# Linear attention through W' = blockdiag(kv) wo and r = pq/den, in a fused transformer block with its gradients

## The chip, the cores and the metric

One Trainium2 chip, one core of it. The kernel is one launch that computes the output of a block and six gradients. The metric is the device time of one execution in microseconds (us); the kernel before takes 846.03 us (median of 3 runs, 845.99 to 848.4). Profiles are of one execution; their span is 1.7 to 1.9 us shorter than the time of the same run.

## The reference

Everything is bf16, S = 2048 rows, D = 640, H = 32 heads of 20 columns, F = 1728.

```python
def A(x, wqkv, wo):                      # linear attention, not causal
    q, k, v = heads(x @ wqkv)
    phi = lambda t: where(t > 0, t + 1, exp(t)) + 1e-6
    pq, pk = phi(q), phi(k)
    kv  = einsum("hsd,hse->hde", pk, v)  # 20 x 20 for each head
    z   = pk.sum(rows)
    num = einsum("hqd,hde->hqe", pq, kv)
    den = einsum("hqd,hd->hq", pq, z) + 1e-6
    return merge(num / den) @ wo

h   = x + A(layernorm(x), wqkv, wo)
out = h + swiglu(layernorm(h), w1, w3, w2)
# returned: out and, for a given grad_out, the gradients of x, wqkv, wo, w1, w3, w2
```

## The kernel before

The program order of every engine is fixed by hand. Rows are handled in 16 tiles of 128. The stages are: setup (layernorm, k, and M = pk^T xn with one more column of ones, which gives z), a fill (the late tiles of q, the first attention tiles), the MLP, its weight gradients, the backward attention with the gradient of h, and last the gradients of wqkv and x. The parts that the change touches:

```python
# fill and MLP: num and den in one product with kvbd (20 columns of kv and 1 of z for each head)
def f2_nd(t):
    for m, a, b, bank, off, first in ND:
        T.matmul(nd[t][bank][:, ...], lhsT=pqT[:, m, tile t], rhs=kvbd[:, m, a * DA:b * DA], ...)
def f2_o(t):                                  # o = num / den, on VectorE
    V.tensor_scalar(out=den, in0=<column of den>, scalar1=1e-6, op0=ALU.add)      # twice
    V.reciprocal(out=rden[:, t, :], in_=den)
    V.tensor_tensor(out=o_t, in0=<num>, in1=rden of the head, op=ALU.mult)         # twice
def f2_ot(t):                                 # o transposed: tiles 0-3 on TensorE, later ones by DMA
    ...
def f2_at(t):                                 # h = x + o wo
    T.matmul(at, lhsT=oT[t][:, c, :], rhs=wo[:, c, half], ...)

def q_late(t):
    pq = p1.tile([P, D], BF16, name="pq", bufs=4)
    ...                                       # two products, ScalarE exp and relu, two VectorE operations
    dma(out=pq_d[tile t], in_=pq)

# backward attention, per tile
def b_go(t):     # g_h wo^T; times rden -> gnd; gnd * o, summed per head -> one more column of gnd
def b_gndT(t):   # gnd transposed
def b_gkv(t):    # gkv += pq^T gnd, five small products, in PSUM over all tiles
def b_gpq(t):    # g_q = phi'(q) * (gnd kvbd^T), six small products
def wo_parts():  # gradient of wo = o^T g_h, stored directly
# last stage: kvbd's gradient transposed by TensorE (13 blocks of 128 x 128), g_v's weights gm,
# g_k and the products for the gradient of wqkv ("jobs"), then the gradient of x
```

Of the kernel before, what the change touches and what calls it, by code (L numbers as in the profile page):

```python
# [9 lines left out]
P = 128  # L10
# [10 lines left out]
DA = DH + 1  # L21
C, CP = H * DA, 768
ST, DT, CT = S // P, D // P, CP // P
# [14 lines left out]
M_W = [(b - a) * DA for a, b in M_H]  # L38
M_MAX = max(M_W)
KV_SLOT = [(0, 0), (0, M_W[0]), (0, M_W[0] + M_W[1]), (1, 0), (1, M_W[3])]  # L40

C_H = [_heads(cc * P, min(C, (cc + 1) * P), DA) for cc in range(CT)]
SPLIT_D, SPLIT_C = 19, 18
# [13 lines left out]
ND = _pieces(M_H, SPLIT_D, DA)  # L57
GP = _pieces(C_H, SPLIT_C, DH)


SQ = _pieces(M_H, SPLIT_D, DH)
SQ_BLOCKS = [(c, [m for m in range(DT) if M_H[m][0] * DH < (c + 1) * P and M_H[m][1] * DH > c * P]) for c in range(DT)]
BLOCKS = [(cc, list(range(a * DH // P, (b * DH - 1) // P + 1))) for cc, (a, b) in enumerate(C_H)]
# [3 lines left out]
def kernel(  # L67
# [34 lines left out]
    pq_d = dram.tile([S, D], BF16, name="pq_d")  # L102
# [3 lines left out]
    o_d = dram.tile([S, D], BF16, name="o_d")  # L106
# [3 lines left out]
    pq_v, pk_v, xn_v, o_v, hn_v, m_v = rows(pq_d), rows(pk_d), rows(xn_d), rows(o_d), rows(hn_d), rows(m_d)  # L110
# [9 lines left out]
    x_ext = U1.tile([P, ST, D + 2], BF16, name="x_sb", tag="S0")  # L120
    x_sb = x_ext[:, :, 0:D]
# [12 lines left out]
    kvbd = cp.tile([P, DT, CP], BF16, name="kvbd")  # L134
# [54 lines left out]
    mask = cp.tile([P, DT, M_MAX], BF16, name="mask")  # L189

    def make_mask(m):
        a, b = M_H[m]
        v = mask[:, m, 0:M_W[m]]
        V.memset(v, 1.0)
        v = v.rearrange("p (h e) -> p h e", e=DA)

        G.affine_select(out=v, in_=v, pattern=[[-DH, b - a], [0, DA]], compare_op=ALU.is_ge, fill=0.0,
                        base=m * P - a * DH, channel_multiplier=1)
        G.affine_select(out=v, in_=v, pattern=[[DH, b - a], [0, DA]], compare_op=ALU.is_gt, fill=0.0,
                        base=a * DH + DH - m * P, channel_multiplier=-1)  # L200

# [12 lines left out]
    def load_pqT(c):  # L214
        dmaT(out=pqT[:, :, c * W:(c + 1) * W], in_=pq_d[c * W:(c + 1) * W, :])

# [8 lines left out]
    pk_all = p1.tile([P, ST, D], BF16, name="pk_all")  # L225
    mT = p1.tile([P, DT, D], BF16, name="mT")
    Z = p1.tile([P, DT], F32, name="Z")
# [37 lines left out]
    def phi(acc, dst, then=None):  # L265

        mq, rq = (p1.tile([P, D], BF16, name=n, bufs=4) for n in ("mq", "rq"))
        A.activation(two(mq[:]), acc[:, :, 0:HD], AF.Exp)
        A.activation(two(rq[:]), acc[:, :, 0:HD], AF.Relu)  # L269

        def rest():
            V.tensor_scalar(out=mq[:], in0=mq[:], scalar1=1.0, scalar2=1e-6, op0=ALU.min, op1=ALU.add)
            V.tensor_tensor(out=dst, in0=mq[:], in1=rq[:], op=ALU.add)
            if then is not None:
                then()
        held.append(rest)
# [5 lines left out]
    def q_store(t, pq):  # L282
        dma(out=pq_v[:, t, :], in_=pq)

    def q_tile(t):
        pq = p1.tile([P, D], BF16, name="pq", bufs=4)
        phi(p1_mm(t, 0), pq[:], lambda: q_store(t, pq[:]))
# [21 lines left out]
    def m_part(m, tiles):  # L309
        if m not in macc:  # L310
            macc[m] = [ps.tile([P, 512], F32, name="macc", tag=("m", "tr")[m % 2], bufs=2) for _ in range(2)]
        for t in tiles:
            for j, n in enumerate((HD, HD + 1)):
                T.matmul(macc[m][j][:, 0:n], lhsT=pk_all[:, t, m * P:(m + 1) * P],  # L314
                         rhs=x_ext[:, t, j * HD:j * HD + n], start=(t == 0), stop=(t == ST - 1))

    def m_end(m):
# [4 lines left out]
        V.tensor_copy(out=Z[:, m:m + 1], in_=acc[1][:, HD:HD + 1])  # L322
# [3 lines left out]
    def kv_block(m, acc):  # L326

        a, b = M_H[m]
        n = (b - a) * DH
        for c in range(DT):  # L330
            T.matmul(acc[:, 0:n], lhsT=mT[:, c, m * P:(m + 1) * P],
                     rhs=wqkv[:, c, 2 * D + a * DH:2 * D + b * DH], start=(c == 0), stop=(c == DT - 1))
        kv, mk = (x[:, m, y].rearrange("p (h e) -> p h e", e=DA)
                  for x, y in ((kvbd, slice(a * DA, b * DA)), (mask, slice(0, M_W[m]))))
        V.tensor_tensor(out=kv[:, :, 0:DH], in0=acc[:, 0:n].rearrange("p (h e) -> p h e", e=DH),
                        in1=mk[:, :, 0:DH], op=ALU.mult)
        V.tensor_scalar(out=kv[:, :, DH], in0=mk[:, :, DH], scalar1=Z[:, m:m + 1], scalar2=None, op0=ALU.mult)

    def zero_pads():
        V.memset(w2T[:, :, F:FP], 0.0)  # L340
        V.memset(x_ext[:, :, D:D + 2], 1.0)
# [38 lines left out]
    for t in range(ST):  # L380
# [11 lines left out]
        phi_rest()  # L392
        phi(k, pk_all[:, t, :])
# [19 lines left out]
    phi_rest()  # L413
    group_out(SC - 1)
    for m in range(DT):
        V.memset(kvbd[:, m, :], 0.0)
        make_mask(m)

    def p1_kv(m):
        kv_block(m, ps.tile([P, 2, 512], F32, name="kvp", tag="big", bufs=2)[:, 0])  # L420
# [5 lines left out]
    m_part(1, (14, 15))  # L426
    m_end(1)
    q_tile(5)
    phi_rest()
    q_tile(6)  # L430
    phi_rest()
    q_tile(7)
    phi_rest()
    m_part(2, range(ST))
    m_end(2)
    m_part(3, range(ST))
    m_end(3)
    load_pqT(0)
    p1_kv(0)
    m_part(4, range(8))  # L440
    p1_kv(1)
    m_part(4, range(8, ST))
    m_end(4)
    load_pqT(1)
    ps.release()
    load_x(0, 2)
    load_x(2, 4)
# [5 lines left out]
    nd, oT, hn, hnT, hhT = {}, {}, {}, {}, {}  # L453

    def f2_nd(t):
        nd[t] = [ps.tile([P, 512], F32, name="nd", bufs=2) for _ in range(2)]
        for m, a, b, bank, off, first in ND:
            a0 = M_H[m][0]
            T.matmul(nd[t][bank][:, off:off + (b - a) * DA], lhsT=pqT[:, m, t * P:(t + 1) * P],
                     rhs=kvbd[:, m, a * DA:b * DA], start=first, stop=True, skip_group_check=True)  # L460

    def f2_o(t):
        o_t = pf.tile([P, D], BF16, name="o_t", bufs=2)
        den = pf.tile([P, H], F32, name="den", bufs=2)
        halves = ((0, SPLIT_D, nd[t][0]), (SPLIT_D, H, nd[t][1]))
        del nd[t]
        seg = [n[:, 0:(b - a) * DA].rearrange("p (h e) -> p h e", e=DA) for a, b, n in halves]
        for (a, b, _), s in zip(halves, seg):
            V.tensor_scalar(out=den[:, a:b], in0=s[:, :, DH], scalar1=1e-6, scalar2=None, op0=ALU.add)
        V.reciprocal(out=rden[:, t, :], in_=den[:])  # L470
        for (a, b, _), s in zip(halves, seg):
            V.tensor_tensor(out=o_t[:, a * DH:b * DH].rearrange("p (h d) -> p h d", d=DH), in0=s[:, :, 0:DH],
                            in1=rden[:, t, a:b].unsqueeze(2).to_broadcast([P, b - a, DH]), op=ALU.mult)
        oT[t] = o_t

    def f2_ot(t):
        if t >= TPC:
            o_t, oT[t] = oT[t], pf.tile([P, DT, P], BF16, name="oT", bufs=2)
            dmaT(out=oT[t][:], in_=o_t[:])
            dma(out=o_v[:, t, :], in_=o_t[:])  # L480
            return
        dma(out=o_v[:, t, :], in_=oT[t][:])
        tr = ps.tile([P, DT, P], BF16, name="tr", bufs=1)
        for c in range(DT):
            T.transpose(tr[:, c, :], oT[t][:, c * P:(c + 1) * P], ident[:])
        oT[t] = pf.tile([P, DT, P], BF16, name="oT", bufs=2)
        A.copy(out=oT[t][:], in_=tr[:])

    def f2_at(t, tag="nd"):
        on_pe = t < 2 * TPC  # L490
        for j in range(2):
# [4 lines left out]
            for c in range(DT):  # L496
                T.matmul(at[:, 0:HD], lhsT=oT[t][:, c, :], rhs=wo[:, c, j * HD:(j + 1) * HD],  # L497
# [7 lines left out]
    def q_late(t):  # L505

        mq, rq = (p1.tile([P, D], BF16, name=n, bufs=4) for n in ("mq", "rq"))
        pq = p1.tile([P, D], BF16, name="pq", bufs=4)
        for j in range(2):
            acc = ps.tile([P, 512], F32, name="mm", bufs=3)  # L510
# [5 lines left out]
        V.tensor_tensor(out=pq[:], in0=mq[:], in1=rq[:], op=ALU.add)  # L516
        q_store(t, pq[:])
# [6 lines left out]
    def f2_ht(t):  # L524
# [7 lines left out]
        tr = ps.tile([P, DT, P], BF16, name="trh", tag="mm", bufs=3)  # L532
# [4 lines left out]
    def mm5(w, fc, rhs):  # L537
        return mm5_to(ps.tile([P, W], F32, name="mm", bufs=3), w, fc, rhs)
# [7 lines left out]
    def mlp_ghh(n):  # L546
        if n < SC * FT:
            ghh_chunk(n, ps.tile([P, W], F32, name="mm", bufs=3))
# [87 lines left out]
    def f2_ndo(t):  # L636
        f2_nd(t)
        f2_o(t)

    FILL = 8  # L640

    def f2_kv(m):
        kv_block(m, ps.tile([P, 512], F32, name="mm", bufs=3))
# [7 lines left out]
    for f, t in ((q_late, 8), (f2_kv, 2), (q_late, 9), (q_late, 10), (f2_kv, 3), (mlp_ghh, 4), (f2_kv, 4), (f2_ndo, 0), (q_late, 11),  # L651
                 (f2_ot, 0), (f2_ndo, 1), (q_late, 12), (f2_at0, 0), (f2_ot, 1), (f2_ndo, 2), (f2_hn, 0), (q_late, 13),
                 (f2_at0, 1), (f2_ot, 2), (f2_ht, 0), (f2_ndo, 3), (f2_hn, 1), (q_late, 14), (f2_x, 4), (f2_at0, 2),
                 (f2_ot, 3), (w2T_rest, 8 * P), (f2_ht, 1), (mlp_ghh, 5), (f2_hn, 2), (f2_at0, 3), (q_late, 15),
                 (f2_ht, 2), (f2_hn, 3), (f2_ndo, 4), (mlp_ghh, 6), (f2_ot, 4), (f2_x, 6), (f2_ht, 3), (load_g2T, 1),
# [643 lines left out]
```

## Time and profile before

| what | us |
|---|---|
| time, median | 846.03 |
| span of the profiled run | 844.2 |
| first matmul of the MLP starts at | 102.5 |
| first product of wo's gradient starts at | 559.7 |
| first product of the jobs on g_q starts at | 587.5 |
| first product of the x gradient starts at | 649.6 |

TensorE is the limit nearly everywhere; the prediction shows the busy table, the slices and the chain. This is TensorE's list of waits; the columns are what waited and for what, then us in total, times, and the longest one.

```profile
PE tr L245 <- DVE x_sb L156: 6.6, 3, 5.4
PE at L497 <- DMA oT<-o_t: 0.7, 1, 0.7
```

Behind the first tiles' layernorm nothing costs TensorE even a microsecond. The next line is a window: bounds, length, busy us and instructions of PE, weight loads, VectorE, ScalarE and GpSimd, then the clock, the share of DMA engines in use and GB/s.

```profile
587.50:649.60 62.10, 61.59 (x497) 45.15 (x495) 29.66 (x46) 13.48 (x34) 0.00 (x0) 1.00 0.81 178
```

### The profile page before, as it was taken

What the parts mean: (1) busy time and instruction counts of PE and PEld (TensorE: products, weight loads), DVE (VectorE), ACT (ScalarE), POOL (GpSimd) and SP (SyncE); (2) the same over time, 40 slices, a digit from 0 to 9 for tenths busy, and PEclk for the clock granted to TensorE, in tenths of its full rate; (3) what the DMA queues carried; (4) which work ended last, traced back from release to release, by engine and by line L of the source; (5) the groups of instructions that cost most, each with busy time, mean ns of one, the idle gap of its engine ahead of it and who ended that gap; (6) DMA issues with size and microseconds to landing.
All of it is one profiled execution on the core that took longest, in us unless ns stands there. A gap on an engine that the chain in (4) does not pass through costs nothing.

```text
span 844.2 us, 14506 instructions
## 1 busy us (share of the span) xinstructions
PE 831.2 (98%) x5719; PEld 534.1 (63%) x5719; DVE 415.0 (49%) x952; ACT 321.0 (38%) x606; POOL 33.3 (4%) x55
## 2 busy tenths in 40 slices
PE   6999999999999999999999999999999999999998
PEld 4667654555555555777777777777777777555554
DVE  7853788778687657400046665662562545200000
ACT  5864877655655666011121112122211333311111
POOL 2310100000000000001000000000000000000000
PEclk9999999999999999999999999999999999999999
DMA  9999799566455457999768789749696688686661
GB/s 263 305 311 231 212 226 262 167 173 173 126 144 148 122 185 211 214 247 267 218 172 188 183 196 218 162 100 239 150 228 116 139 205 178 137 184 147 162 165 37
DMA packets 341156, 158.57 MB, mean 188 GB/s; under 512 B 241760, under 2 KB 339808, under 8 KB 341088
## 3 DMA queue, kind: packets, MB, share of 16 engines
q1 hardware_dynamic: 312272, 144.67, 69.3%
q10 hardware_dynamic: 28816, 12.97, 6.7%
q8 instruction: 45, 0.74, 0.4%
q14 instruction: 23, 0.19, 0.1%
HBM read 48.64 MB, written 50.32 MB: 117 GB/s over the span
## 4 chain that ended last, share of the span: by engine, by line
PE 95%; DMA 2%; DVE 2%; ACT 1%; issue 0%; SPq 0%; DVEq 0%; ACTq 0%
PE mm L293 19%; PE job L1093 19%; PE ghn L858 14%; PE gxn L1226 8%; PE o L622 7%; PE gw L797 7%; PE big L251 4%; PE at L497 3%; PE macc L314 3%; PE gwo L965 3%; PE h L915 3%; PE dkv L1173 2%; DMA x_sb<-in_A_x_dram 1%; PE mm L251 1%; PE h L946 1%; PE gkv L938 1%
## 5 line engine op out<-in xcount | busy, mean ns | idle before, releaser
L1093 PE MATMUL job<-gb,hnN 128*128 128x432 bf16 x640 | 117.0, 346 | 0.0
L858 PEld LDWEIGHTS <-ggb 128*128 128x128 bf16 x864 | 83.1, 98 | 30.9
L1093 PEld LDWEIGHTS <-hnN 128*128 128x128 bf16 x640 | 62.6, 98 | 54.1
L293 PE MATMUL mm<-pqT,w 128*128 128x512 bf16 x405 | 95.6, 379 | 0.0
L293 PEld LDWEIGHTS <-w 128*128 128x128 bf16 x540 | 52.5, 98 | 60.5
L1097 ACT CAST obs<-job 128x432 bf16<-128x432 f32 (+1 forms) x60 | 29.1, 485 | 134.8 <-PE job L1093 134.8
L622 PE MATMUL o<-w,hhT 128*128 128x320 bf16 x448 | 67.5, 299 | 0.0
L858 PE MATMUL ghn<-w13a,ggb 128*128 128x320 bf16 x448 | 65.6, 299 | 0.0
L293 PE MATMUL mm<-g2T,w2T 128*128 128x512 bf16 x260 | 64.6, 379 | 0.2 <-ACT up L570 0.2
L858 PE MATMUL ghn<-w13b,ggb 128*128 128x320 bf16 x416 | 63.5, 299 | 0.0
L622 PEld LDWEIGHTS <-hhT 128*128 128x128 bf16 x448 | 43.8, 98 | 23.6
L797 PE MATMUL gw<-g,hb 128*128 128x320 bf16 x416 | 57.7, 299 | 0.0
L881 ACT ACTIVATE y<-wb,s,ln_rs 128x640 bf16<-128x640 f32 x32 | 29.4, 920 | 66.5 <-DVE wb L877 66.5
L303 ACT CAST ghh<-mm 128x512 bf16<-128x512 f32 x52 | 30.5, 586 | 55.3 <-PE mm L293 53.9
L797 PEld LDWEIGHTS <-hb 128*128 128x128 bf16 x416 | 40.3, 98 | 15.3
L1226 PE MATMUL gxn<-wqT,gT 128*128 128x320 bf16 x320 | 48.7, 299 | 0.0
L869 ACT ACTIVATE gs<-ghn 128x640 bf16<-128x640 f32 x16 | 11.2, 703 | 87.4 <-PE ghn L858 87.4
L562 ACT ACTIVATE sig<-mm 128x512 bf16<-128x512 f32 x56 | 33.5, 598 | 28.3 <-PE mm L293 26.0
L293 PEld LDWEIGHTS <-w2T 128*128 128x128 bf16 x280 | 27.2, 98 | 25.4 <-issue 0.5
L251 PEld LDWEIGHTS <-pqT 128*128 128x128 bf16 x320 | 31.7, 101 | 14.9 <-issue 1.4
L251 PE MATMUL big<-wqkv,pqT 128*128 128x320 bf16 x240 | 38.7, 314 | 0.3 <-ACT rq L269 0.2
L1093 PEld LDWEIGHTS <-g 128*128 128x128 bf16 x320 | 31.2, 98 | 12.3 <-issue 0.3
(158 smaller groups left out, 1157.3 us busy)
## 6 DMA issues: line engine op xcount, KB each, us to landing
hh_d<-hhT SPq DMA_DIRECT2D x24, 256.0 KB, 2.6
gg_d<-gate SPq DMA_DIRECT2D x24, 256.0 KB, 2.6
gg_d<-up SPq DMA_DIRECT2D x24, 256.0 KB, 2.5
ggb<-gg_d SPq DMA_DIRECT2D x6, 896.0 KB, 6.1
ggb<-gg_d SPq DMA_DIRECT2D x6, 832.0 KB, 7.7
out_dram<-obs ACTq DMA_DIRECT2D x40, 108.0 KB, 2.2
ggb<-gg_d SPq DMA_DIRECT2D x2, 1728.0 KB, 12.4
x_sb<-in_A_x_dram SPq DMA_DIRECT2D x5, 640.0 KB, 4.9
```

The lines of the kernel that those rows point to most:

```text
L251: T.matmul(acc, lhsT=pqT[:, c, t * P:(t + 1) * P], rhs=wqkv[:, c, n0:n0 + HD], start=(c == 0), stop=(c == DT - 1))
L293: T.matmul(acc[:], lhsT=w[:, c, fc * P:(fc + 1) * P], rhs=rhs[:, c, :], start=(c == 0), stop=(c == DT - 1))
L303: A.copy(out=ghh[n // 2][:, n % 2, :], in_=acc[:])
L314: T.matmul(macc[m][j][:, 0:n], lhsT=pk_all[:, t, m * P:(m + 1) * P], rhs=x_ext[:, t, j * HD:j * HD + n], start=(t == 0), stop=(t == ST - 1))
L562: A.activation(sig[:, i, :], gp[:], AF.Sigmoid)
L622: T.matmul(o2["ps"][:, 0:HD], lhsT=hhT[c][:, fc, i * P:(i + 1) * P], rhs=w2[:, fc, j * HD:(j + 1) * HD], start=(fc == 0), stop=(fc == FT - 1))
L797: T.matmul(acc[:, j, 0:HD], lhsT=hb[b][:, t, i * P:(i + 1) * P], rhs=g2[:, t, j * HD:(j + 1) * HD], start=(t == 0), stop=(t == ST - 1))
L858: T.matmul(acc[:, j, 0:HD], lhsT=ggb[t // 2][:, k, lo:lo + P], rhs=rhs[:, j * HD:(j + 1) * HD], start=(k == 0), stop=(k == NG - 1))
L881: A.activation(out=y[:], in_=wb[:], func=AF.Identity, bias=s[:, 3:4], scale=st.rs[:, t:t + 1])
L1093: T.matmul(acc[:, 0:n], lhsT=lhs[:, t, m * P:(m + 1) * P], rhs=rhs(t), start=(t == 0), stop=(t == ST - 1))
L1097: A.copy(out=ob, in_=acc[:, 0:n])
L1226: T.matmul(acc[:, j, 0:HD], lhsT=g, rhs=wqT[:, k, j * HD:(j + 1) * HD], start=(k == 0), stop=(k == 14))
```

## The change

The intent is to take matmuls and transpositions out of TensorE's stream. In the code `dma` is a plain transfer and `dmaT` a transposing DMA, a transfer that transposes on its way; both are issued by one queue, that of SyncE (the SP queue). As (num/den) wo = r W' with r = pq/den and W' = blockdiag(kv) wo, one small product for W' replaces num for every tile, and den is made outside TensorE: GpSimd multiplies pq by z, VectorE sums per head. Backward, one product g_h W'^T gives g_r. The gradient of wo is blockdiag(kv)^T (r^T g_h), the gradient of kv comes from the diagonal blocks of wo (r^T g_h)^T, and that of z from 32 more columns beside g_h. The core of the diff:

```diff
+    def z_add(t):                                  # z on GpSimd, tile by tile in the setup loop
+        G.tensor_tensor(out=zs[:], in0=zs[:], in1=pk_all[:, t, :], op=ALU.add)
+    def r_prod(t):
+        for j in range(2):
+            G.tensor_tensor(out=pr[t, j][:], in0=pqs[t][:, js], in1=Zb[:, js], op=ALU.mult)
+    def r_rest(t):
+        for j in range(2):
+            V.reduce_sum(out=den[:, j * 16:(j + 1) * 16], in_=heads(pr.pop((t, j))[:]), axis=AX.X)
+        V.tensor_scalar(out=den[:], in0=den[:], scalar1=1e-6, scalar2=None, op0=ALU.add)
+        V.reciprocal(out=rden[:, t, :], in_=den[:])
+        V.tensor_tensor(out=heads(pqs[t][:]), in0=heads(pqs[t][:]), in1=<rden of the head>, op=ALU.mult)
+    def r_out(t):
+        dmaT(out=pqT[:, :, t * P:(t + 1) * P], in_=pqs[t][:])
+        dma(out=r_v[:, t, :], in_=pqs.pop(t)[:])
...
-    def f2_nd(t): ...   def f2_o(t): ...   def f2_ot(t): ...
-                T.matmul(at[:, 0:HD], lhsT=oT[t][:, c, :], rhs=wo[:, c, j * HD:(j + 1) * HD],
+                T.matmul(at[:, 0:HD], lhsT=pqT[:, c, t * P:(t + 1) * P], rhs=Wp[:, c, j * HD:(j + 1) * HD],
     def q_late(t):
-        pq = p1.tile([P, D], BF16, name="pq", bufs=4)
+        pqs[t] = pf.tile([P, D], BF16, name="pql", bufs=4)
...
+    def f2_wT(i):                                  # W', transposed, in five row blocks
+    def f2_Wp():
+        for i in range(DT):
+            dmaT(out=Wp[:, :, i * P:(i + 1) * P], in_=wTs[0][:, i, :])
...
-    def b_go(t): ...   def b_gndT(t): ...   def b_gkv(t): ...   def b_gpq(t): ...
+    def b_gr(t):    # g_r = g_h W'^T; VectorE: times r, summed per head; GpSimd: times z
+    def b_gq(t):    # VectorE: g_q = (g_r - s z) * min(r, rden)
...
+    for i in range(DT):                            # last stage: gradient of wo
+        dwoT.append(br.tile([P, D], BF16, name="dwoT", bufs=2))
+        unload(square(qp, kvN, i), dwoT[i][:], (A.copy, V.tensor_copy)[i % 2])
+        dmaT(out=dwo[:, :, i * P:(i + 1) * P], in_=dwoT[i][:])
+    A.dma_start(out=out3S, in_=dwo[:])
...
-    for c, ms in SQ_BLOCKS:                        # kv's gradient transposed by TensorE
-        ...T.transpose(tr[:, i, :], gkv_b[:, m, c * P:(c + 1) * P], ident[:])
     for i in range(DT):
         unload(square(wqT[:, 2 * DT:, :], gkvT, i), gm[:, i, :], (A.copy, V.tensor_copy)[i % 2])
         dmaT(out=wqT[:, 2 * DT:, i * P:(i + 1) * P], in_=gm[:, i, :])
+    for m in range(DT):                            # ... now by DMA, behind gm's
+        dmaT(out=gkv_b[:, :, m * P:(m + 1) * P], in_=gkvT[:, m, :])
```

The program order of the fill is new as well: r of tiles 0 to 11 is made before the MLP, r of tiles 12 to 15 in its first chunk.

## The prediction

> **What bounds the kernel now.** I read the busy table first, then the 40 slices, then the chain of work that ended last.
>
> ```profile
> PE 831.2 (98%) x5719; PEld 534.1 (63%) x5719; DVE 415.0 (49%) x952; ACT 321.0 (38%) x606; POOL 33.3 (4%) x55
> ...
> PE   6999999999999999999999999999999999999998
> ...
> DVE  7853788778687657400046665662562545200000
> ...
> PE 95%; DMA 2%; DVE 2%; ACT 1%; issue 0%; SPq 0%; DVEq 0%; ACTq 0%
> ```
>
> TensorE is busy 98% of 844.2 us and is 95% of the chain, so TensorE time removed is time saved, provided nothing new makes it wait. VectorE has room on average (49%), but the slices show 7s and 8s early on. So I read the windows by stage next: setup to 54 us, the last products of pk and xn (54 to 74), a fill stage that makes the rest of q, the first attention tiles and the first normalised rows (74 to 102.5), then the MLP.
>
> ```profile
> 54.00:74.00 20.00, 19.97 (x151) 14.23 (x150) 7.41 (x27) 8.02 (x17) 4.16 (x10) 1.00 1.07 294
> 74.00:102.50 28.50, 27.57 (x235) 19.28 (x232) 21.08 (x68) 22.26 (x53) 2.37 (x4) 1.00 0.82 205
> ```
>
> Columns: window, length, busy us of PE, PE loads, DVE, ACT, POOL, then clock, DMA share, GB/s. In the fill stage VectorE is already at 21.1 of 28.5 us and TensorE loses under 1 us. Then the chain in the backward attention stage, one tile of rows:
>
> ```profile
> 435.63 6.11 PE ghn L858 x45
> 441.75 0.33 PE gkv L938 x5
> 442.08 1.22 PE ghn L858 x9
> 443.30 1.36 PE h L915 x10
> ```
>
> Ten 320-column matmuls advance the chain by 1.36 us (136 ns each); five small gkv ones cost 0.33 us. Small products are cheap singly but there are many.
>
> [...] 492 ns for a bf16 add of 640, 820 for a reduce of 640, 822 for an fp32 add of 640. [...]
>
> **The change, TensorE's work.** The order listing has 256 fewer matmuls. Removed, with pitches from TensorE's timeline: nd, 16 tiles x 0.35 = 5.6 us; gkv, 16 x 0.33 = 5.3; the g_q product, 16 x 0.35 = 5.6; 57 transposes (o, gnd, kvbd) at 56 ns = 3.2. Together 19.7. Added: two sets of 30 block products (W', wo gradient) and 25 (kv gradient), 85 x 58 ns = 4.9; the sum of z, 4 x 0.136 = 0.5; 80 matmuls that are 32 columns longer, 80 x 13 ns = 1.1. Together 6.5. **Net 13.2 us less.** From the MLP on it is: nd of tiles 5 to 15, 3.9; gkv, g_q and gnd transposes 11.6; kvbd transposes 1.4; minus 1.1 and 3.2 of additions; plus 0.7 us of an existing wait for a transposed o. So 13.3 us less after 102.5 us, if no stall is added there.
>
> In the backward stage VectorE per tile goes from 6.1 us (2 x 0.49 + 0.51 + 0.82 + 0.24 + 2 x 0.48 + 2.56 for the layernorm) to 6.9 (five passes of 0.82 instead of those, 0.2, and 2.56), against a TensorE tile of 9.37 - 0.68 = 8.7 us. It still fits; that saving I count in full.
>
> **The change, setup and fill.** Here r for every tile needs a chain that was not there: GpSimd multiplies pq by Zb [...], VectorE reduces twice (0.41 pitch each), adds, inverts and scales (0.2 + 0.38 + 0.82): 2.2 us against 1.5 for nd's division before. Then a transposing DMA and a store. Three new waits follow.
>
> First, z. GpSimd must add the last pk tile, then it still has the ten mask operations in its queue (54.85 to 59.35 us before), and only then zl. I get zl at about 61.5, while TensorE reaches the z sum at 57.9: 3.6 us lost.
>
> Second, kv. With the roles of the operands swapped, block m needs the transposed M block m+1. Block 2 is asked for 2.5 us after M's block 3 is finished, but copying it (0.75) and its transposing DMA (median 3.7 in the DMA table) take 4.5: 2 us lost.
>
> Third, and largest: **the pql buffers.** There are four, and the order listing shows that the add that writes pq of tile 9 waits for two DMA semaphores: the transposition and the store of r of tile 5. Tile 10 waits for tile 6, up to tile 15 for tile 11. In VectorE's order the scaling of r of tile 6 stands directly before the add of tile 10, so VectorE stops until two DMAs have been issued and have landed. What that costs is in the SP queue's timeline of before:
>
> ```profile
> 111.41 1.20 SPq L479 DMA_TRANSPOSE oT<-o_t  x1
> 112.66 0.58 SPq L480 DMA_DIRECT2D o_d<-o_t  x1
> ```
>
> The transposition occupies the queue 1.25 us and the store (2.2 us to landing, DMA table) starts after it: 3.5 us from r to free buffer. One tile's round is thus 2.2 (r) + 3.5 (DMAs) + 0.5 (the add) = 6.2 us, and six rounds (r of tiles 6 to 11) 37 us. Statistics and normalisations (1.3 + 0.44 per tile, four tiles) partly hide in the waits; I count 6 us of them as extra. Before the first round the queue also carries the five transpositions of W' (5 x 1.23), two stores (2 x 0.6) and then tile 5's pair (3.5): about 10 us after W' has been copied out. TensorE, in order, waits for the normalised rows of tiles 0 to 3, which stand behind these adds.
>
> My clock for it: z sum 61.5; M's products end 76 (73.9 before, with 4.1 us of q work moved behind); q 5 to 8 and kv to 82; W' copies, behind r of tile 5 on VectorE, end 89; tile 9's add at 98.6; tile 12's at 117; tile 15's at 142; MLP starts at 144 instead of 102.5. That is 41 us. Some steps may overlap better than I drew them, so I take **37 us**. Sum: 846.0 - 13.3 + 37 = 869.7, rounded to **869**.
>
> **Rivals.** (a) TensorE remains the bound throughout and the waits hide: 846 - 13 = 833, at best 829 if present waits vanish as well. For it: 98% busy now, and the new order looks carefully placed. Against: VectorE's and the queue's own sums in the fill stage exceed TensorE's 29 us. (b) VectorE's work alone is the limit, the buffers not: from the first r at 64 us it has 12 x 2.2 + 11 x 0.82 + 4 x 1.75 + 4 for W' and masks = 46 us, so the MLP starts near 112: total 843. (c) [...] GpSimd's multiplications [...] stretch VectorE's operations in the backward stage as well: VectorE would pass 8.7 us per tile; each 0.5 us over adds 8 us, on top of either. (d) The wo and kv gradients, now a serial train of transposing DMAs, stall TensorE before its last stages; 6 us of other jobs lie between the copy and the use of the last block, against 3.8 needed, so I expect under 1 us.
>
> **Range and chances.** The buffer wait is read from the program, its length from DMA times of the trace; I am about three quarters sure that it dominates, which gives 860 to 880. The rest lies with (a) and (b), 833 to 850, and mixtures. Range 845 to 882. Faster by over 2% means below 829, under the whole saving without a single new stall: 0.04. Within 2% (829 to 863): 0.25. Slower: 0.71.
>
> **What would show it.** Right: a fill stage with TensorE well under half busy; VectorE waiting for DMA before the add that writes pql, six or seven times by about 3 us and once by 8 or more; GpSimd between z's last add and zl; the MLP's first matmul near 140 us; after it every stage no longer than before, the backward tile at 8.7 us. Wrong: if that add waits under 1 us, (a) or (b) holds; if the backward tile stays at 9.4 or more, (c) does.

## The result, and the profile after

The changed kernel takes 921.5 us (median of 4 runs, 918.92 to 923.91), the kernel before in the same rounds 846.56. The ratio is 1.088, 95% interval 1.0853 to 1.0907. It is slower by 75 us, where 23 were predicted. All outputs are right. These are the busy table, three rows of slices and the chain by engine of the changed kernel.

```profile
PE 838.3 (91%) x5463; PEld 527.0 (57%) x5463; DVE 454.1 (49%) x921; ACT 322.6 (35%) x619; POOL 101.0 (11%) x119
...
PE   6987615999999999999999999998669999999998
...
DVE  7967254689677675650015777771236245500000
...
PEclk9999857999999999999999999999779999999999
...
PE 73%; DVE 7%; SPq 5%; DMA 3%; issue 2%; ACT 2%; DVEq 0%; ACTq 0%
```

TensorE has 256 fewer matmuls and yet more busy time. Its clock fell in two places (slices of 5 and 7); in e14 below, without the long waits, the clock stays at 1.0 and the busy time at 822.3 us. The holes in TensorE's row are in the same two places, about 60 to 160 us and 650 to 690 us. TensorE makes up 73% of the chain, not 95%: VectorE, the SP queue (SPq) and DMA waits fill the rest. By stage, start times from TensorE's timeline:

| first product of | before | after | difference |
|---|---|---|---|
| MLP | 102.5 | 161.8 | +59.3 |
| w2's gradient | 354.3 | 412.8 | +58.6 |
| backward attention (g_h times wo^T or W'^T) | 434.1 | 492.0 | +57.9 |
| wo's gradient | 559.7 | 608.8 | +49.1 |
| jobs on g_q | 587.5 | 635.9 | +48.4 |
| x gradient | 649.6 | 727.5 | +77.9 |
| end of the span | 844.2 | 922.1 | +77.9 |

So 59 us are lost before the MLP, 11 are won from there to the jobs, most of them (8.8) in the backward attention, and 29.5 are lost in the stage of 62 us that follows. These are the windows of the two bad stages (columns as above).

```profile
74.00:102.50 28.50, 22.90 (x168) 15.53 (x167) 17.11 (x39) 13.58 (x37) 6.20 (x8) 0.88 0.53 120
102.50:161.80 59.30, 22.45 (x126) 13.38 (x125) 26.05 (x64) 13.49 (x32) 9.22 (x13) 0.68 0.44 104
```
```profile
635.90:727.50 91.60, 70.85 (x539) 50.59 (x537) 31.95 (x52) 15.65 (x40) 0.00 (x0) 0.87 0.81 172
```

In the 59 us before the MLP no engine is busy even half of the time: that is the sign of waits. TensorE's waits name who ended them:

```profile
PE trh L558 <- DVE hn L145: 36.9, 3, 27.0
PE dkv L1120 <- ACT dwoT L1089: 10.7, 2, 7.5
PE dkv L1083 <- DMA bd<-small: 8.9, 4, 5.8
PE tr L236 <- DVE x_sb L145: 7.7, 3, 5.4
PE zp L295 <- POOL zl L288: 3.1, 1, 3.1
```

The first is TensorE waiting for the normalised rows that VectorE makes behind its own waits. The second and third, 19.6 us, are nearly the whole of the last stage's 20.2 us of new idle time. The third is for bd, the transposed gradient of kv, behind this train in the SP queue's timeline (wqT<-small, which is gm's, took 9.79 us between the two, and 6.69 us before the change):

```profile
646.52 10.10 SPq L1097 DMA_TRANSPOSE dwo<-dwoT  x5
...
673.52 6.51 SPq L1135 DMA_TRANSPOSE bd<-small  x5
```

VectorE's list says what it waited for in the fill:

```profile
DVE pql L522 <- DMA r_d<-pql: 33.5, 7, 12.6
```

Seven waits of the add that writes pql, for the store of an earlier r, 33.5 us in all. The SP queue's timeline before the first of them (start, duration, what), and VectorE's timeline at it, where the brackets give the idle time and who ended it:

```profile
95.54 6.48 SPq L539 DMA_TRANSPOSE Wp<-wTs  x5
102.08 0.58 SPq L540 DMA_DIRECT2D wT_d<-wTs  x1
102.71 0.52 SPq L541 DMA_DIRECT2D kvT_d<-bd  x1
103.27 2.68 SPq L320 DMA_TRANSPOSE pqT<-pql  x1
106.00 1.33 SPq L321 DMA_DIRECT2D r_d<-pql  x1
```
```profile
98.63 0.33 DVE L521 TENSOR_SCALAR mq<-mq 128x640 bf16<-128x640 bf16 x1 [2.71 <-ACT mq L519]
111.60 0.49 DVE L522 TENSOR_TENSOR pql<-mq,rq 128x640 bf16<-128x640 bf16 x1 [12.64 <-DMA r_d<-pql]
```

Tile 5's buffer, scaled at 93.5, waits behind the five transpositions of W' and two stores, and is free only at 111.6. In the backward attention, on the other hand, the tiles follow each other as intended:

```profile
509.39 1.52 PE L920 MATMUL gr<-wT,ghT 128*128 128x320 bf16 x10
510.75 2.61 PE L864 MATMUL ghn<-w13b,ggb 128*128 128x320 bf16 x18
513.19 3.97 PE L864 MATMUL ghn<-w13a,ggb 128*128 128x320 bf16 x28
517.00 1.25 PE L864 MATMUL ghn<-w13b,ggb 128*128 128x320 bf16 x8
518.08 1.52 PE L920 MATMUL gr<-wT,ghT 128*128 128x320 bf16 x10
```

From 509.39 to 518.08 is 8.69 us for a tile, without a wait.

### The profile page after: what moved, and what is told of

It reads as the page before. It is cut to its first block, busy times and chain, and to the rows that moved or that the text cites. A ratio compares the mean times of both kernels' runs of the same rounds, so it can differ in the third digit from the quotient of the medians. Undisturbed runs are those within 1.5% of the kernel's fastest.

```text
span 922.1 us, 13964 instructions
## 1 busy us (share of the span) xinstructions
PE 838.3 (91%) x5463; PEld 527.0 (57%) x5463; DVE 454.1 (49%) x921; ACT 322.6 (35%) x619; POOL 101.0 (11%) x119
## 4 chain that ended last, share of the span: by engine, by line
PE 73%; DVE 7%; SPq 5%; DMA 3%; issue 2%; ACT 2%; DVEq 0%; ACTq 0%
PE job L1053 17%; PE mm L327 15%; PE ghn L864 13%; PE gxn L1203 7%; PE o L646 6%; PE gw L816 6%; PE gr L920 2%; PE dkv L1150 2%; DMA r_d<-pql 2%; PE at L503 1%; SPq L971 1%; DVE den L313 1%; SPq L320 1%; DMA dwo<-dwoT 1%; DVE s L622 1%
## 5 line engine op out<-in xcount | busy, mean ns | idle before, releaser
L327 PE MATMUL mm<-pqT,w 128*128 128x512 bf16 x405 | 95.9, 383 | 1.8 <-ACT gate L588 0.9
L864 PE MATMUL ghn<-w13a,ggb 128*128 128x320 bf16 x448 | 63.5, 299 | 0.0
L864 PE MATMUL ghn<-w13b,ggb 128*128 128x320 bf16 x416 | 61.4, 299 | 0.0
L887 ACT ACTIVATE y<-wb,s,ln_rs 128x640 bf16<-128x640 f32 x32 | 29.5, 921 | 66.5 <-DVE wb L883 66.5
L337 ACT CAST ghh<-mm 128x512 bf16<-128x512 f32 x52 | 30.6, 588 | 57.4 <-PE mm L327 48.9
L928 POOL TENSOR_TENSOR sz<-Zb,g_h 128x640 f32<-128x640 bf16 x16 | 20.2, 1262 | 271.3 <-DVE g_h L926 271.3
L142 POOL TENSOR_TENSOR ln_rs<-ln_ve,mhalf 128x1 f32<-128x1 f32 x32 | 23.6, 736 | 202.3 <-DVE ln_ve L140 202.1
L242 PEld LDWEIGHTS <-pqT 128*128 128x128 bf16 x320 | 33.5, 107 | 17.6 <-DMA pqT<-x_sb 1.1
```

What stands on the lines that cost most here:

```text
L142: G.tensor_tensor(out=self.rs[:, a:b], in0=self.ve[:, a:b], in1=mhalf[:, 0:b - a], op=ALU.pow)
L242: T.matmul(acc, lhsT=pqT[:, c, t * P:(t + 1) * P], rhs=wqkv[:, c, n0:n0 + HD], start=(c == 0), stop=(c == DT - 1))
L327: T.matmul(acc[:], lhsT=w[:, c, fc * P:(fc + 1) * P], rhs=rhs[:, c, :], start=(c == 0), stop=(c == DT - 1))
L337: A.copy(out=ghh[n // 2][:, n % 2, :], in_=acc[:])
L864: T.matmul(acc[:, j, 0:HD], lhsT=ggb[t // 2][:, k, lo:lo + P], rhs=rhs[:, j * HD:(j + 1) * HD], start=(k == 0), stop=(k == NG - 1))
L887: A.activation(out=y[:], in_=wb[:], func=AF.Identity, bias=s[:, 3:4], scale=st.rs[:, t:t + 1])
```

## The experiments

The theory after this: (1) the four pql buffers, each tied to a transposing DMA and a store, cost the larger part of the fill; (2) what is left of the fill is VectorE's own work on r; (3) the last stage is lost to the new transposing DMAs of wo's and kv's gradients. The rivals: the fill is bound by VectorE whatever the buffers; GpSimd and VectorE hinder each other; the last stage is bound by copies and reused buffers, and not by transfers.

### e1_pql: buffers for three more tiles of pq

```diff
-        pqs[t] = pf.tile([P, D], BF16, name="pql", bufs=4)
+        pqs[t] = wTs["slot"][:, DT + t - 9, :] if 9 <= t < 12 else pf.tile([P, D], BF16, name="pql", bufs=4)
```

The slot is the dead space behind W'.

> Change: pq of tiles 9 to 11 is written into the unused rest of the slot that holds W', so no add of pq waits for the two DMAs of a tile four earlier. Theory A (the buffer round through two DMAs makes the fill stage long): the seven waits of the add that writes pql for r's store (33.5 us in all in the changed kernel) fall below 5 us, and the MLP's first matmul moves from 161.8 us to 120-128 us; total 880-890 us. Rival B (VectorE's own work in the fill stage is the limit, the waits only fill its idle time): VectorE stays busy to about 155 us and the total stays within 5 us of 921. Rival C [...]: the VectorE operations between the waits lengthen as GpSimd multiplies more densely, and under half of the 33 us comes back.

894.15 us, ratio 1.0564 (1.0535 to 1.0593): 27 us won with one small edit, though 4 us above the expected range. The MLP starts at 132.6 instead of 161.8. VectorE's waits at that add are down to 1.6 us, and TensorE's wait for the rows to:

```profile
PE trh L560 <- DVE hn L145: 12.8, 3, 8.0
```

So the buffers are the largest single cause, 29 us of the 59; rival C, under half of 33 us back, does not hold. The start came later than expected: with the waits gone, VectorE is busy for 43.4 of the 58.6 us from 74 to 132.6, so its work probably sets the pace for a good part of the rest.

### e2_store: the store of r on ScalarE's queue

```diff
-        dma(out=r_v[:, t, :], in_=pqs.pop(t)[:])
+        A.dma_start(out=r_v[:, t, :], in_=pqs.pop(t)[:])
```

> Change: only the store of r goes to ScalarE's queue, so that it is issued beside the transposition and not 1.25 us after it. Theory A: each of the seven waits of the pql add shrinks by about 0.8-1.2 us (to the 2.6 us of the transposition), the first one by as much, the fill stage by 6-8 us; total 913-916 us, if ScalarE's queue, which then waits for r in order, does not hold up its own work. Rival B: no change (within 2 us of 921) since VectorE's work is the same.

917.77 us, ratio 1.0844 (1.0828 to 1.086). The add's waits fell from 33.5 to 20.8 us, but a store in ScalarE's stream holds up ScalarE until r is ready:

```profile
DVE pql L522 <- DMA pqT<-pql: 20.8, 7, 10.6
```
```profile
PE mm L327 <- ACT rq L520: 12.8, 1, 12.8
```

The first line is from VectorE's list, the second from TensorE's: a new wait of 12.8 us. Only 4 us are won, short of the 6 to 8 expected of the fill. Moving the transfer to an engine that computes moved a part of the wait with it.

### e3_dwoT: five buffers for the wo gradient's blocks instead of two

```diff
-        dwoT.append(br.tile([P, D], BF16, name="dwoT", bufs=2))
+        dwoT.append(br.tile([P, D], BF16, name="dwoT", bufs=2) if i < 2 else
+                    br.tile([P, 2 * D], BF16, name="dwoT2", tag=("cc", "pb", "sz")[i - 2])[:, 0:D])
```

> Change: the five transposed pieces of the wo gradient get five buffers instead of two. Theory A' (the second loss, about 20 us before the k gradient stage, is the copies of these pieces that wait for the DMA of the piece two before, while TensorE waits for their PSUM): the 11.4 us of TensorE's wait on the copies go; but the transposes of the product Q are queued behind two large loads and land near 648 us, so 5-6 us of a wait for them appear in place; total 914-917 us. Rival B' (the DMA queue's order alone sets it): total stays within 2 us of 921. The 8.9 us wait for the transposed kv gradient stays in both.

920.41 us, ratio 1.0876 (1.0846 to 1.0906), a miss. The wait on dwoT is gone and this one stands in its place:

```profile
PE dkv L1121 <- DVE small L193: 9.4, 1, 9.4
```

The three slots that I took lie in memory that the buffer of kv's gradient reuses a moment later, so its clearing by GpSimd waited for the same transfers. That was a fault of my placement.

### e5_d: e3 with kv's transposing DMAs ahead of gm's, and two loads of xn later

The diff is that of e3, with the last loop of the diff above moved before the one over i and two loads moved behind both.

> Change: e3 and in addition the transposes of the kv gradient are issued before those of gm, and the two large loads of xn are issued after both. Theory A': TensorE's idle time between the first job on g_q and the gxn stage falls from 20.8 us to under 3 us; total 901-905 us. If only the copies were the cause it equals e3.

912.76 us, ratio 1.0779 (1.0752 to 1.0807), a miss: less won than expected. The wait on bd, 8.9 us, is gone; e3's fault is still in it, as GpSimd's timeline shows:

```profile
646.94 2.76 POOL L1113 MEMSET small<- 128x3200 bf16 x1 [24.07 <-DMA dwo<-dwoT]
```

### e4_bd: only the order of kv's transposing DMAs

> Only the order of the transposing DMAs changes: the five of kv's gradient are issued ahead of g_m's five. Theory (a long serial train of transposing DMAs on one queue delays the small gradients): PE's 8.9 us wait of kv's gradient on bd falls below 1 us, the 10.7 us wait for the dwo buffer stays, time 912 to 915. Rival (these waits only change places, since the queue is just as full): another wait of 5 us or more on the same queue appears and the time stays within 919 to 924.

916.03 us, ratio 1.0822 (1.0802 to 1.0842), 1 us off the expected range. The wait on bd fell from 8.9 to 1.1 us, the one on dwoT stayed (11.3): 5.5 of the 8 us were won, and no new wait of 5 us came, so the rival did not hold here either.

### e7_d2: the last stage without e3's fault

The three more buffers lie in an output buffer that is idle; in addition, kv's transposing DMAs come first, the loads of xn later, and wo's store goes to the SP queue.

```diff
+        dwoT.append(br.tile([P, D], BF16, name="dwoT", bufs=2) if i < 2 else obs[:, i * D:(i + 1) * D])
-    A.dma_start(out=out3S, in_=dwo[:])
+    dma(out=out3S, in_=dwo[:])
```

> Repairs the last stage alone: three more buffers for the dwo blocks in memory that nothing asks for again there, kv's gradient transposes first, the two last loads of xn after g_m's loop, one output store moved to another queue. Theory: PE waits between the wo gradient and the x gradient fall from about 20 us to under 3 us and the time to 900 to 905. Rival (that stage is also bound by ScalarE and GpSimd copies): over 8 us of PE waits remain and the time is 908 or more.

912.04 us, ratio 1.0778 (1.0749 to 1.0807), a miss: the rival's side. The wait on dwoT is gone, but that on bd is back with 9.4 us.

### e9_fill: the fill alone

```diff
+        pqs[t] = pqm[0][:, t - 8, :] if 8 <= t < 12 else pf.tile([P, D], BF16, name="pql", bufs=4)
...
-            if c == 0 and fc >= 2 and fc < 14:
+            if c < 2 and fc >= 2 and fc < 14:       # r of tiles 8 to 15 in the MLP's chunks 0 and 1
                 u, k = divmod(fc - 2, 3)
-                (r_prod, r_rest, r_out)[k](12 + u)
+                (r_prod, r_rest, r_out)[k](8 + 4 * c + u)
```

The masks and the clearing of bd also moved into the setup loop, and the stores of W' and kv behind r's transfers.

> Repairs the fill alone: pq of tiles 8 to 11 written into an idle slot, so that no tile waits for another's transposition; r of tiles 8 to 15 formed in the first two chunks of the MLP; memsets and stores that nobody waits for moved. Theory (buffer waits plus VectorE's added work in the fill make the 59 us): first MLP matmul at 105 to 115 us instead of 162, time 865 to 878, with some 2 to 4 us given back in the first chunks. Rival (VectorE's r work has no room beside the MLP either): the MLP stage grows by 10 us or more and the time is above 885.

875.68 us, ratio 1.0337 (1.032 to 1.0353), in the expected range. The MLP starts at 117.4 (a little later than expected) and takes 250.1 us to w2's gradient, against 251.1 in the changed kernel: r's work costs nothing there. With e1 this says of the fill: of 59.3 us, 44.4 are buffer waits and work that can stand elsewhere. How much each of e9's edits brings was not separated.

### e8_all: e9 and e7 together

> Both repairs together. If the fill and the last stage are the whole loss and independent, the gains add: 921.5 less about 50 and less about 18 is 845 to 858, that is within 2% of the kernel before, on either side. If PE's saving of 13 us is real it can come out under 846. Rival (something else in the change costs time too): it stays above 865.

866.35 us, ratio 1.0232 (1.0207 to 1.0258). Above the expected range and on the rival's side by 1 us: up to the jobs on g_q it is level with the kernel before (587.3 against 587.5), and then the last stage takes 81.7 us instead of 62.1. It still waits on bd for 8.5 us.

### e12_zafter: z on TensorE

The changed kernel, with z as 32 products with ones instead of GpSimd's additions.

```diff
-        z_add(t - 1)
...
-            for i, z in enumerate((zh, zl)):
-                T.matmul(acc[:, j, 0:HD], lhsT=ones[:], rhs=z[:, j * HD:(j + 1) * HD], ...)
+            for t in range(ST):
+                T.matmul(acc[:, j, 0:HD], lhsT=ones[:], rhs=pk_all[:, t, j * HD:(j + 1) * HD], ...)
```

> The changed kernel with one thing undone in kind: z is summed on TensorE (32 products with a matrix of ones, 4.4 us at 136 ns) instead of sixteen additions on GpSimd. Theory [...] (rival c of the prediction, seen so far only in the setup loop, where VectorE's additions of 640 take 0.85 to 1.3 us instead of 0.49): VectorE's operations there go back to about 0.49 us and VectorE's busy time from 36 to 62 us falls by 8 us or more; the wait on zl (3.1 us) goes; the time moves by only -1 to -4 us because the buffer waits of the fill follow anyway. Rival (VectorE is slower there for another reason): durations stay over 0.8 us and the time rises by 1 to 4 us.

918.58 us, ratio 1.0851 (1.0833 to 1.0869). These are the groups of VectorE's operations from 36 to 62 us (line, names, shapes and count, then busy us and mean ns of one), of the changed kernel and of this run:

```profile
L264 DVE TENSOR_TENSOR pk_all<-mq,rq 128x640 bf16<-128x640 bf16 x9 | 7.6, 845 | 0.9
...
L264 DVE TENSOR_TENSOR pq<-mq,rq 128x640 bf16<-128x640 bf16 x4 | 5.3, 1316 | 0.4
```
```profile
L264 DVE TENSOR_TENSOR pk_all<-mq,rq 128x640 bf16<-128x640 bf16 x8 | 3.9, 492 | 1.8 <-ACT rq L260 1.6
...
L264 DVE TENSOR_TENSOR pq<-mq,rq 128x640 bf16<-128x640 bf16 x4 | 2.0, 493 | 0.7 <-ACT rq L260 0.5
```

The same addition takes 492 ns where GpSimd does not add, and means of 845 and 1316 ns where it does (its own additions take 1404 ns); VectorE's busy time from 36 to 62 us falls from 23.3 to 13.0 us, and the wait on zl is gone, as expected. That GpSimd's additions cause the longer ones is shown, by what mechanism is not. The effect is small here, net of 3.8 us of added products on TensorE: the MLP starts 4.5 us earlier (157.3), and about 3 us of it reach the end.

### e10_d3 and e11_z: stores and loads on GpSimd's queue; z on TensorE

In e10_d3 (e8 with the edit below) wo's store and the first two loads of pk go to GpSimd's queue. In e11_z z is made on TensorE too.

```diff
-    dma(out=out3S, in_=dwo[:])
+    G.dma_start(out=out3S, in_=dwo[:])
-        dma(out=pkb[c][:], in_=pk_v[...])
+        (G.dma_start if c < 2 else dma)(out=pkb[c][:], in_=pk_v[...])
```

> Both repairs, and in the last stage the store of wo's gradient and the first two loads of pk go to GpSimd's queue, so that the transposing DMAs of kv's gradient follow those of dwo without a gap. Theory (what is left in that stage, 8.5 us of waiting on bd, is still the one queue's order): the wait falls below 2 us and the time from 866 to 854 to 859. Rival (the transposing DMAs themselves take that long): bd's wait stays above 5 us and the time above 861.

> The kernel before this one with z summed on TensorE too. [...] this gains 2 to 6 us net of the 3.8 us of added products: 850 to 856. If not, it is 0 to 4 us slower.

865.2 us, ratio 1.0226 (1.0203 to 1.0248), and 866.93 us, 1.0241 (1.0224 to 1.0257). Both missed. In e10 the wait on bd went, and one of 12.0 us on VectorE's masking of kv's gradient came: the clearing of that buffer stands behind the store in GpSimd's stream. In e11 the products added to TensorE cost about what GpSimd's additions had cost; the difference of 1.7 us lies within the intervals.

### e13_d4: e10 with that buffer cleared by VectorE

```diff
-    G.memset(gkvT, 0.0)
+    V.memset(gkvT, 0.0)
```

> The run before last but with one edit: kv's gradient buffer is cleared by VectorE, not by GpSimd, whose queue now holds the store of dwo and so cleared it 12 us late. Theory (all of the last stage's loss is queue order): TensorE's 12.0 us wait on VectorE's masking disappears, the stage from the first g_q product to the first x gradient falls from 82 to 72 us or less, and the time from 865 to 853 to 858. Rival (the transposing DMAs are too many to hide in any order): a wait of 5 us or more on bd or on the x^T loads comes in its place and the time stays above 860.

864.26 us, ratio 1.0153 (1.0115 to 1.019); the kernel before was slow on this chip (849.95), so the time by itself says little. The trace is on the rival's side: the stage takes 85.0 us, and TensorE's wait moved once more.

```profile
PE dkv L1084 <- DMA bd<-small: 14.5, 3, 9.0
```
```profile
out_dram<-dwo POOLq DMA_DIRECT2D x1, 800.0 KB, 8.5
...
bd<-small SPq DMA_TRANSPOSE x5, 11.5
```

The second fence is from the list of transfers from 585 to 640 us (what, queue, count, KB, median us from issue to landing). The transpositions of bd, now early, take 11.5 us to land instead of 2.6 in the changed kernel, and hold the SP queue for 13.96 us instead of 6.51. Six arrangements of this stage (e3, e5, e4, e7, e10, e13) had each removed a wait that they aimed at, and none had won more than 10.4 of its 29.5 us. This left two causes: the order together with reused buffers, or the ten added transposing DMAs as such.

### e15_pe_after and e14_pe: those ten transpositions on TensorE

e15_pe_after is the changed kernel, e14_pe is e8, each with this edit (e15 also has e7's five dwoT buffers, which it needs):

```diff
-        dmaT(out=dwo[:, :, i * P:(i + 1) * P], in_=dwoT[i][:])
+    for i in range(DT):
+        tr = d_tr(DT)                                  # in PSUM
+        for c in range(DT):
+            T.transpose(tr[:, c, :], dwoT[i][:, c * P:(c + 1) * P], ident[:])
+        (A.copy, V.tensor_copy)[i % 2](out=dwo[:, :, i * P:(i + 1) * P], in_=tr[:])
...
-        dmaT(out=gkv_b[:, :, m * P:(m + 1) * P], in_=gkvT[:, m, :])
+    for c, ms in SQ_BLOCKS:                            # 13 blocks, as in the kernel before
+        for i, m in enumerate(ms):
+            T.transpose(tr[:, i, :], gkvT[:, m, c * P:(c + 1) * P], ident[:])
+        V.tensor_copy(out=gkv_b[:, c, ...], in_=tr[:])
```

> The changed kernel with the ten transposing DMAs of dwo and of kv's gradient replaced by 38 transpositions of 128x128 on TensorE (56 ns each, 2 us) and copies out of PSUM. Theory (the transposing DMAs are the cause, by their number): TensorE's waits in the last stage before the x gradient fall from 20 us to under 5 us, the stage from 91.6 to 74 to 78 us, the time from 921 to 903 to 908. Rival (buffers and copies hold it up whatever transposes): over 10 us of waits remain and the time is 911 or more.

> The same replacement in the version with the fill repaired and the loads reordered (866 us). Theory: its wait on bd of 8.5 us goes, the stage takes 66 to 70 us instead of 82, and the time is 850 to 856. Rival: the stage stays above 75 us and the time above 860.

904.84 us, ratio 1.0691 (1.0672 to 1.071), and 851.87 us, ratio 1.0066 (1.0048 to 1.0084); both in the expected ranges. In e15 the stage takes 75.6 us instead of 91.6. Its waits do not fall below 5 us as expected, for the largest that remains in it is for five other transposing DMAs, those of r^T g_h:

```profile
PE dkv L1128 <- DMA tri<-tri: 5.5, 2, 4.0
```

In e14 the stage takes 69.1 us instead of e8's 81.7. Its window (columns as above) and the page's busy table are

```profile
585.65:654.70 69.05, 67.24 (x576) 49.98 (x574) 34.18 (x59) 17.49 (x43) 0.00 (x0) 1.00 0.90 201
```
```profile
PE 822.3 (97%) x5501; PEld 520.4 (61%) x5501; DVE 459.6 (54%) x928; ACT 324.1 (38%) x622; POOL 103.1 (12%) x119
```

e14 and e8 have the same buffers and loads and differ in these ten (and in the moment of dwo's store, which follows them). So the ten added transposing DMAs cause 12.6 us of the 19.6 that e8 still loses in the last stage. Six orders of them did not repair it; that none would have is not shown. Whether five of the ten, dwo's or bd's, would have been enough was not tried. Whether the queue that issues them one by one or the DMA engines behind it run out first was not separated either: the share of DMA engines in use is 0.88 in e8's stage and 0.90 in e14's.

### e18_z and e16_best: what is left of the fill

e18_z is e14 with z's last five tiles summed on TensorE. e16_best is e18 with r of tile 7, and all later ones, in the MLP's first chunk; one pql buffer more, and one less of the kind that holds GpSimd's products and the MLP's output rows.

> The version with the ten transpositions on TensorE, and z's last five tiles summed by TensorE (ten products of 0.136 us) instead of GpSimd. [...] the net gain is 1 to 3 us: 849 to 851. If not, 852 to 854.

> The same, and r of tile 7 moved into the MLP's first chunk with tiles 8 to 15, where VectorE has room; one buffer more for pq and one less of the kind that GpSimd's products use. If VectorE's work (2.7 us a tile) sets the end of the fill: another 1 to 3 us, 846 to 850, level with the kernel before. If the MLP's first chunk has no room for nine tiles, 852 or more.

852.05 us, ratio 1.006 (1.0045 to 1.0074): nothing won. 864.74 us, ratio 1.0214 (1.0192 to 1.0235): 13 us lost. In e16 TensorE waits in the MLP for ScalarE's copies, up to 3 us at a time:

```profile
PE mm L330 <- ACT ghh L340: 7.0, 4, 3.0
```

From 110 to 160 us it is busy for 41.8 us, in e18 for 48.9. Nine tiles of r are more than the first chunk holds beside its own work, or the buffer taken away is missed there; these two were changed together and stay unseparated. No version that I built beats the kernel before. The best two, e14_pe and e18_z, are 0.6 to 0.7% slower.

## Why the prediction was right or wrong

That it would be slower was right; by how much was not. 23 us were predicted and 75 measured. The step that failed is the overlap in rival (d): the new transposing DMAs of the last stage were put at under 1 us, and that stage lost 29.5 us. The fill, with the right mechanism, was mis-sized: it lost 59.3 us instead of 37. The saving on TensorE was 2 us smaller than predicted.

- **TensorE's work, right to about 2 us.** Predicted net 13.2 us less. At full clock e14 has 822.3 us against 831.2, with 38 transpositions (38 x 56 ns = 2.1 us) that the change does not have: 11.0 less. The 13 ns for 32 more columns were an estimate; measured are 313 ns for 352 columns and 299 for 320. The stretch from the MLP to the jobs alone gave 59.3 - 48.4 = 10.9, where 13.3 were predicted from the MLP on.
- **The backward tile, right.** 8.7 us predicted, 8.69 measured. Rival (c) does not hold in that stage: VectorE's five new passes over 640 elements are at 818 to 825 ns there.
- **The first two waits of setup, right in kind.** z: 3.6 predicted, 3.1 measured. The transposed M blocks: 2 predicted, 3.4 measured (two waits of 3.0 us together, and one of 0.4).
- **The pql buffers, right in mechanism, too small by 18 us in my clock and by 22 in the sum.** The add that writes pql waited seven times, once for 12.6 us and else for 2 to 5. A round was 7.8 us on average (111.60 to 158.21 for six) against 6.2, but with the extras that I had added the rounds were 46.6 against 43.4. The term that was missed is the one ahead of them, "W' copies, behind r of tile 5 on VectorE, end 89; tile 9's add at 98.6": the copies ended at 95.9 and the add ran at 111.6. TensorE's small W' products waited for their copies and masks several times (4.4 us in all), and the pair of transfers of tile 5 took 8.3 us from its first issue, not 3.5. The MLP started at 161.8, not 144. I then wrote 37 us where my own clock said 41, hoping for overlap; the stage took longer instead.
- **Rival (b), the second bound.** That VectorE's own work alone starts the MLP near 112 is close to the 112.5 to 117.4 of the versions without buffer waits, although those have some of r's work moved into the MLP. With all of it left in the fill (e1) the start was 132.6, so this sum was probably too small as well. One term of it was: r took VectorE 2.7 us per tile (112.01 to 114.71 for tile 6), not 2.2. e1 still has short waits of other kinds.
- **Rival (c), placed in the wrong stage.** GpSimd's additions of z stretch VectorE's additions in the setup loop (492 to 1316 ns). It costs about 3 us in the end (e12). I had counted z's additions as one wait at their end, and not as company for VectorE. (In the setup of the kernel before GpSimd has short operations on 128x1, 0.2 to 0.9 us each, and VectorE's additions stay at 492 ns there.)
- **Rival (d), the overlap that failed.** "6 us of other jobs lie between the copy and the use of the last block, against 3.8 needed, so I expect under 1 us." The stage lost 29.5 us. By its windows 20.2 are idle time; 5.7 are the lower clock, and 3.5 the small products themselves, net of the transpositions that went (estimates: 70.9 busy here against some 65.1 in e14's stage without its transpositions, and 61.6 before). I had compared one block's latency with one gap. What counts is the train: dwo, gm, bd and r^T g_h bring 20 transposing DMAs on one queue, where the kernel before had gm's five beside its transposing loads, and two dwoT buffers tie TensorE to them. Ten of them taken away bring 12.6 us in the stage where the buffers stay the same (e14 against e8), and 16 us together with five dwoT buffers (e15).
- **The clock was in no step.** The mean clock was 0.68 from 102.5 us to the MLP and 0.87 in the last stage, and 1.0 in the same two stages of e14, without the long waits. What set the clock is not shown beyond these means; in the last stage the lower clock came to 5.7 us on top of 20.2 of idle time (the estimates above).

## What to carry to other kernels

When work leaves TensorE, follow every buffer that the replacement writes to the event that frees it, and add up the queue ahead of that event: a buffer that is free only after a transposing DMA and a store costs a round trip per tile (8.3 us for tile 5 here), and one more buffer for each of a few tiles can be worth more than all the matmuls saved (29 us against 11 here). Count the transposing DMAs of a stage as a sum and not one by one: five in a row, of 160 KB each, held the queue for 6.48 us here, and a plain store of 160 KB for 0.58 in the kernel before. A handful of transpositions on TensorE can be far cheaper where the queue is already full: 38 of them, at 56 ns for each 128x128 block, in place of ten transposing DMAs won 12.6 us of the last stage (e14 against e8). And when moving one wait only brings up the next, stop reordering and take work away.
